# A mixture-of-experts and cosine block on one core: chains across engines spread over steps, conversions let in by a booked budget, the square on ScalarE

## The chip, the core and the metric

The kernel runs on one core of a Trainium2 chip. A core has a matrix engine (TensorE, PE in the rows; its weight loads are PEld), a vector engine (VectorE, DVE), an engine for activation functions (ScalarE, ACT), a general engine (GpSimd, POOL) and SyncE (SP), which here issues most transfers. Each engine takes its own instructions in order; a semaphore makes one wait for another. The metric is the time of one execution on the device in microseconds (us).

## The reference, cut to what matters

```python
scores = q @ k.T / 8 + bias            # 4 batches, 8 heads, 576 positions, 64 wide
x = softmax(scores) @ v                # -> 2304 tokens of 512
e = argmax(x @ w_gate)                 # one of 8 experts per token
y = gate * relu(x @ w1[e]) @ w2[e]     # 512 -> 1024 -> 512
h = y @ w_in                           # 512 -> 2048
out = (h * cos(h)) @ w_out             # 2048 -> 512
```

The weights `w_in` and `w_out` arrive as 64-bit floats and are turned into 32-bit ones on the chip.

## The kernel before

Three blocks follow each other: attention, the expert block (`moe_dense`), and the last block (`moe2`). To keep 32-bit precision each operand of a large product is split into a rounded high half (`h`) and a remainder, the low half (`l`), and a product is three matmuls: high by high, high by low, low by high.

**Expert block.** For each of the four batches `b` the expert that most of its tokens chose is applied to all of its 576 tokens; tokens of one other expert are gathered, computed apart and added (`Extra`). A batch has two halves `hf` of 288 tokens, a half eight hidden chunks `f`, so `seq` has 64 steps `s`. A step runs `layer1` of its chunk (12 matmuls into `pl`, of which there are two buffers, then ScalarE makes the high half `hh` and VectorE the low half `hl`) and `layer2` of the chunk two steps earlier (12 matmuls into `po`). Between them other work is issued, in a written-out order. `later.add` puts functions on step numbers, `later.step` runs those that are due, at the end of a step; `later.drip` takes single instructions out of a long chain of small ones (the gate's choice of experts, the choice of the extra group). That other work is:

- `split`: the high half of a quarter of a weight on ScalarE and at once its low half on VectorE, eight per batch.
- `split_x`: for the next half of tokens, the product of the activations with the gate factor `Cb` on GpSimd, the rounding on ScalarE, the subtraction on VectorE, all at once, two of four chunks at `f` = 3 and two at `f` = 4. For the very first half the product runs on VectorE, chunk by chunk, when the block opens.
- `cv.half`: half of the conversion of one piece of a 64-bit weight. The two halves of a piece are four VectorE instructions, then an addition on GpSimd and a transfer out. 40 pieces fall into this block, two halves in every step that a fixed condition lets through.
- `extra.add` (four steps per batch from step 48) adds the gathered tokens' result on VectorE; `split_group` at step 57 splits the first tokens of the last block.

**Last block.** Six groups `g` of 384 tokens, sixteen hidden chunks `f` each: 96 steps. A step runs `layer1` (12 matmuls into `ph`) and `layer2` of four steps earlier (9 matmuls into `py`). In between stands the chain of `h cos h`: ScalarE `turns` (the multiple of a full turn, `tk`), VectorE three instructions of `reduce` (L1267 to L1269), ScalarE the sine of half the angle (L1334), VectorE two instructions of `cosine` (L1274: -2 s s; L1275: (r + 1) h), ScalarE the high half `gh`, GpSimd the low half `gl` (L1344). The angle is taken at the step itself, reduction and sine one step later, the rest two steps later. In the first steps the second half of the weights (quarters 4 to 7) is still to be split: `split_w`, the high half on ScalarE, the low half on GpSimd. The next group's tokens are split at `f` = 8 to 11, the low half also on GpSimd.

## Time and profile before

| what | value |
|---|---|
| median of 3 runs | 1027.79 us (1026.69 to 1029.92) |
| the profiled execution | 1027.14 us, its span 1025.4 us |
| TensorE busy | 981.6 us, 96% of the span |
| VectorE, ScalarE, GpSimd busy | 780.5, 524.4, 363.0 us |
| mean granted TensorE clock | 0.986 |
| expert block, first matmul to the last block's first | 343.84 to 608.54 us |
| last block | from 608.54 us |

A row of the trace gives the line of the kernel, the engine, the operation, the tile written and those read (`hl<-pl,hh`), the shape, how often it came, and its times. The idle time of an engine stands in brackets with what ended it. A stretch's row gives each engine's busy time and number of instructions, the granted clock as a share of the full 2.4 GHz, and what transfers moved.

### The profile page before, as it was taken

What the parts mean: (1) busy time and instruction counts of PE and PEld (TensorE: products, weight loads), DVE (VectorE), ACT (ScalarE), POOL (GpSimd) and SP (SyncE); (2) the same over time, 40 slices, a digit from 0 to 9 for tenths busy, and PEclk for the clock granted to TensorE, in tenths of its full rate; (3) what the DMA queues carried; (4) which work ended last, traced back from release to release, by engine and by line L of the source; (5) the groups of instructions that cost most, each with busy time, mean ns of one, the idle gap of its engine ahead of it and who ended that gap; (6) DMA issues with size and microseconds to landing.
All of it is one profiled execution on the core that took longest, in us unless ns stands there. A gap on an engine that the chain in (4) does not pass through costs nothing. (4 is left out here: it accounts for less than half of the span.)

```text
span 1025.4 us, 17745 instructions
## 1 busy us (share of the span) xinstructions
PE 981.6 (96%) x6369; PEld 821.0 (80%) x6370; DVE 780.5 (76%) x1588; ACT 524.4 (51%) x1123; POOL 363.0 (35%) x408
## 2 busy tenths in 40 slices
PE   8989999999999898998999899999999999999996
PEld 4467777776666597998889897799999999999995
DVE  8977777778667578657448679988878779788774
ACT  8877878787776433325225355443334333333332
POOL 2655454556451122211212106733324224232221
PEclk9999999999999898999999999999999999999998
DMA  8974646664535384734556733101010010100000
GB/s 261 318 251 161 205 135 224 209 199 131 165 124 170 122 263 149 232 83 152 166 197 208 234 135 113 41 3 60 1 62 1 1 62 1 62 1 2 31 1 35
DMA packets 63886, 127.41 MB, mean 124 GB/s; under 512 B 6904, under 2 KB 21516, under 8 KB 63788
## 3 DMA queue, kind: packets, MB, share of 16 engines
q1 hardware_dynamic: 62860, 123.66, 37.1%
q0 software_dynamic: 640, 2.36, 0.8%
q8 instruction: 52, 0.85, 0.3%
q14 instruction: 46, 0.38, 0.1%
q10 hardware_dynamic: 288, 0.16, 0.1%
HBM read 92.55 MB, written 33.60 MB: 123 GB/s over the span
## 5 line engine op out<-in xcount | busy, mean ns | idle before, releaser
L1344 POOL TENSOR_TENSOR gl<-tg,gh 128x384 fp32r<-128x384 f32 x96 | 97.3, 1014 | 289.4 <-ACT gh L1343 289.3
L1262 ACT ACTIVATE tk<-ph,magic 128x384 f32<-128x384 f32 x96 | 55.6, 579 | 204.8 <-PE ph L1323 204.8
L1323 PE MATMUL ph<-xh,w0l 128*128 128x384 f32 x384 | 129.5, 337 | 0.0
L1323 PE MATMUL ph<-xh,w0h 128*128 128x384 f32 x384 | 129.2, 336 | 0.0
L1323 PE MATMUL ph<-xl,w0h 128*128 128x384 f32 x384 | 129.2, 336 | 0.0
L703 POOL TENSOR_TENSOR f32a<-f32a,raw 128x256 f32<-128x256 f32 x64 | 47.5, 742 | 205.9 <-DVE raw L701 120.1
L1269 DVE SCALAR_TENSOR_TENSOR tr<-tk,tr 128x384 f32<-128x384 f32 x96 | 116.6, 1215 | 3.3
L1358 PE MATMUL py<-w1h,gl 128*128 128x512 f32 x288 | 113.9, 395 | 3.0 <-POOL gl L1344 3.0
L1358 PE MATMUL py<-w1h,gh 128*128 128x512 f32 x288 | 113.5, 394 | 1.2 <-ACT gh L1343 1.2
L1358 PE MATMUL py<-w1l,gh 128*128 128x512 f32 x288 | 112.8, 392 | 0.0
L538 ACT ACTIVATE e<-s,mn 128x576 f32<-128x576 f32 x128 | 98.5, 770 | 20.0 <-DVE mn L527 17.3
L527 DVE CUSTOM_DVE_ANT_0 s<-ps_s,Bp 128x576 f32<-128x576 f32 x112 | 84.2, 753 | 30.6 <-PE ps_s L511 26.3
L596 PE MATMUL pa<-eT,V 128*64 128x256 f32 (+3 forms) x640 | 103.1, 425 | 0.6 <-ACT eT L565 0.6
L559 PE MATMUL Tp<-ident,e 128*128 128x128 f32 x576 | 87.4, 275 | 3.0 <-DVE eT L567 1.1
L824 PE MATMUL pl<-xh,w0h 128*128 128x288 f32 x256 | 82.1, 321 | 7.7 <-DVE hl L829 5.8
L510 PE MATMUL ps_s<-HI 128*128 128x288 f32 x256 | 84.2, 345 | 2.3 <-DVE mn L527 2.0
L1274 DVE SCALAR_TENSOR_TENSOR tr<-tr 128x384 f32<-128x384 f32 x96 | 82.2, 856 | 0.0
L824 PE MATMUL pl<-xl,w0h 128*128 128x288 f32 x256 | 78.0, 305 | 0.3
L510 PEld LDWEIGHTS ps_s<-HI 128*128 128x128 f32 x256 | 48.5, 189 | 36.7 <-issue 14.9
L824 PE MATMUL pl<-xh,w0l 128*128 128x288 f32 x256 | 77.3, 302 | 0.0
L842 PE MATMUL po<-hh,w1h 128*128 128x288 f32 x256 | 76.5, 299 | 0.0
L842 PE MATMUL po<-hl,w1h 128*128 128x288 f32 x256 | 76.4, 298 | 0.0
(213 smaller groups left out, 2473.0 us busy)
## 6 DMA issues: line engine op xcount, KB each, us to landing
Bp<-in_w SPq DMA_DIRECT2D x38, 512.0 KB, 4.7
Rqk<-in_qk SPq DMA_DIRECT2D x32, 576.0 KB, 6.1
Bd<-ev SPq DMA_DIRECT2D x36, 295.5 KB, 4.5
raw<-in_w_in SPq DMA_DIRECT2D x32, 256.0 KB, 4.4
raw<-in_w_out SPq DMA_DIRECT2D x32, 256.0 KB, 2.9
X<-xT SPq DMA_DIRECT2D x7, 1152.0 KB, 5.7
Bp<-Bd SPq DMA_DIRECT2D x21, 288.0 KB, 6.7
V<-in_v SPq DMA_DIRECT2D x16, 320.0 KB, 4.3
```

Source lines behind the costliest of these rows:

```text
L510: nc.tensor.matmul(ps[:, hf, :HF], w, HI[:, par, 1, sl], start=True, stop=False)
L527: nc.vector.tensor_tensor_reduce(out=h2(s), in0=d["ps"][:, :, :HF], in1=h2(bias(hp, i)), scale=-0.125, scalar=3e38, op0=ALU.add, op1=ALU.m ...
L538: nc.scalar.activation(out=e[:, par, :], in_=s, func=AF.Exp, bias=mn, scale=-1.0, accum_out=sm[b][:, qt, par, hp:hp + 1])
L559: nc.tensor.transpose(Tp[:, k, :], e[:, par, k * 128:(k + 1) * 128], ident)
L596: nc.tensor.matmul(pa[64 * par:64 * par + 64, :W], V[rows, k, par, :], eT[rows, k, par, :W], start=(k == 0), stop=(k == 4))
L824: nc.tensor.matmul(ps[:, :HF], w[:, c, :], x[:, c, :], start=(n == 0), stop=(n == 3 * NP_ - 1))
L842: nc.tensor.matmul(self.acc[d][:, :HF], w[:, ds_], x, start=(f == 0 and n == 0), stop=(f == self.FC - 1 and n == 2))
L1269: nc.vector.scalar_tensor_tensor(out=r, in0=k, scalar=-PI2B, in1=r, op0=ALU.mult, op1=ALU.add)
L1274: nc.vector.scalar_tensor_tensor(out=r, in0=r, scalar=-2.0, in1=r, op0=ALU.mult, op1=ALU.mult)
L1323: nc.tensor.matmul(ps[:, :GT], w[:, c, :], x[:, c, :], start=(n == 0), stop=(n == 3 * NP_ - 1))
L1344: nc.gpsimd.tensor_tensor(out=lo, in0=g, in1=hi.bitcast(F32), op=ALU.subtract)
L1358: nc.tensor.matmul(acc[t], x[:, ts_], w, start=(f == 0 and n == 0), stop=(f == FC - 1 and n == 2))
```

## The change

In the expert block `split` and `split_x` are cut into parts. The high half is issued in one step and the low half in the next. The product with the gate factor becomes a function of its own, `weigh`, on GpSimd, at `f` = 3 and 4 as before; rounding follows at `f` = 4, 5, subtraction at `f` = 5, 6. The first half's four products move into the last attention pair, on GpSimd. The conversions lose their fixed condition. Every piece of VectorE's work is booked in `dense.cost` with a written price, a half conversion of 0.73 is issued from step 3 on as long as the sum stays at or under `STEP` = 3.1, and 3.1 is taken off at the end of each step.

In the last block the low halves of the weights go to VectorE, one step behind the high half, and their loads and splits are three steps apart where they were two. The subtraction of the next group's tokens stays on GpSimd, a step after the rounding. The square runs on ScalarE after the sine; VectorE then makes (s s - 1/2) h in one instruction, and the output copies multiply by -2. Angle and reduction are issued a step after the first layer, sine and square two steps after it, cosine and split three; the second layer still follows four steps after the first. The output copy of each third of the tokens is issued straight after its matmuls.

```diff
@@ attention, last pair
+                if t - 15 * NTL in (2, 3, 4, 6):
+                    dense.weigh(0, 0, (2, 3, 4, 6).index(t - 15 * NTL), 1, nc.gpsimd)
@@ class Dense
-    def split(self, b, which, q):
-        nc = self.tc.nc
-        src = self.raw.pop((b, which, q))
+    def split(self, b, which, q, part=None):
+        nc = self.tc.nc
         hi, lo = self.w[which, q]
-        nc.scalar.activation(out=hi, in_=src, func=AF.Copy)
-        nc.vector.tensor_tensor(out=lo, in0=src, in1=hi.bitcast(F32), op=ALU.subtract)
+        src = self.raw[b, which, q]
+        if part != 1:
+            nc.scalar.activation(out=hi, in_=src, func=AF.Copy)
+        if part != 0:
+            nc.vector.tensor_tensor(out=lo, in0=src, in1=hi.bitcast(F32), op=ALU.subtract)
+            self.cost += 1.23
+            del self.raw[b, which, q]
...
+    def weigh(self, b, hf, c0, n, eng):
+        src = self.xT[:, c0:c0 + n, b, hf * HF:(hf + 1) * HF]
+        eng.tensor_tensor(out=src, in0=src, in1=self.gate.Cb[b][:, hf * HF:(hf + 1) * HF].unsqueeze(1).to_broadcast(
+            [128, n, HF]), op=ALU.mult)
...
-        (nc.vector if first else nc.gpsimd).tensor_tensor(
-            out=src, in0=src, in1=self.gate.Cb[b][:, t].unsqueeze(1).to_broadcast([128, n, HF]), op=ALU.mult)
-        nc.scalar.activation(out=hi, in_=src, func=AF.Copy)
-        nc.vector.tensor_tensor(out=lo, in0=src, in1=hi.bitcast(F32), op=ALU.subtract)
+        if part == 0:
+            nc.scalar.activation(out=hi, in_=src, func=AF.Copy)
+        else:
+            nc.vector.tensor_tensor(out=lo, in0=src, in1=hi.bitcast(F32), op=ALU.subtract)
+            self.cost += 0.38 * n
@@ moe_dense
+        def convert(least):
+            while cv and cv.u < cv.end and (dense.cost + 0.73 <= STEP or least > 0):
+                cv.half()
+                dense.cost += 0.73
+                least -= 1
...
-                if s < 5:
-                    dense.split(0, *((1, 1), (0, 2), (0, 3), (1, 2), (1, 3))[s])
-                if f in (3, 4) and (hf == 0 or b + 1 < B):
-                    dense.split_x(b + hf, 1 - hf, (f - 3) * 2, 2)
+                if hf == 0 or b + 1 < B:
+                    nx = b + hf, 1 - hf
+                    if f in (3, 4):
+                        dense.weigh(*nx, (f - 3) * 2, 2, nc.gpsimd)
+                    if f in (4, 5):
+                        dense.split_x(*nx, (f - 4) * 2, 2, 0)
+                    if f in (5, 6):
+                        dense.split_x(*nx, (f - 5) * 2, 2, 1)
...
+                dense.cost += 0.6 * bool(later.chains)
-            if cv and s >= 3 and s % 8 != 1 and not 19 <= s <= 23 and (s < 48 or s % 4 != 1):
-                cv.half()
-                cv.half()
+            if s >= 3:
+                convert(2 if s >= len(seq) else 0)
+            dense.cost = max(0.0, dense.cost - STEP)
@@ moe2
-            nc.gpsimd.tensor_tensor(out=lo, in0=src, in1=hi.bitcast(F32), op=ALU.subtract)
+            dense.split(B, which, q, 1)
...
+        def sines(s):
+            r = d[s]["r"]
             nc.scalar.activation(out=r, in_=r, func=AF.Sin, scale=0.5)
+            nc.scalar.activation(out=r, in_=r, func=AF.Square)
...
-            cosine(nc, g, d[s]["r"], d[s]["h"])
+            nc.vector.scalar_tensor_tensor(out=g, in0=d[s]["r"], scalar=0.5, in1=d[s]["h"], op0=ALU.subtract,
+                                           op1=ALU.mult)
...
-                        nc.scalar.activation(out=o, in_=acc[t], func=AF.Copy)
+                        nc.scalar.activation(out=o, in_=acc[t], func=AF.Copy, scale=-2.0)
...
-                    later.add([(2 * i + 2 + j, lambda q=q, j=j: dense.load(B, j, q, True))])
-                later.add([(2 * i + 4 + j, lambda q=q, j=j: split_w(q, j))])
+                    later.add([(3 * i + 1 + j, lambda q=q, j=j: dense.load(B, j, q, True))])
+                later.add([(3 * i + 3 + j + k, lambda q=q, j=j, k=k: split_w(q, j, k)) for k in range(2)])
...
-            later.step()
...
-                angles(s)
-            if 0 <= s - 1 < N:
-                reduced(s - 1)
-            if 0 <= s - 2 < N:
-                cosines(s - 2)
-                split_g(s - 2)
+            for lag, work in ((3, cosines), (1, angles), (1, reduced), (2, sines), (3, split_g)):
+                if 0 <= s - lag < N:
+                    work(s - lag)
+            later.step()
...
+                if f in (9, 10, 11, 12):
+                    lower_x(g + 1, f - 9)
```

## Rows read from the trace of the kernel before

**Rows 1.** Stretches, columns: length, busy PE, PEld, DVE, ACT, POOL; clock; transfer share; GB/s

```profile
343.84:608.54 264.70, 247.95 (x1754) 234.72 (x1755) 178.57 (x407) 96.75 (x187) 48.66 (x53) 0.96 0.56 181
...
621.07:662.06 40.99, 36.73 (x169) 29.54 (x168) 39.71 (x40) 19.91 (x34) 30.88 (x18) 1.00 0.31 96
662.06:1004.51 342.45, 342.45 (x1723) 310.96 (x1722) 283.13 (x424) 130.95 (x277) 106.26 (x101) 1.00 0.06 22
```

**Rows 2.** The same stretches, instructions on tile ph alone

```profile
621.07:662.06 40.99, 18.13 (x96) 17.04 (x96) 8.82 (x16) 4.49 (x8) 1.00 0.31 96
662.06:1004.51 342.45, 185.80 (x984) 174.61 (x984) 93.15 (x168) 48.26 (x83) 1.00 0.06 22
```

**Rows 3.** The chain that ended last, 585 to 600 us: start, us, what

```profile
589.71 1.58 PE pl L824 x12
591.29 1.59 PE po L842 x12
```

**Rows 4.** Waits of PE, expert block: us, times, longest

```profile
PE pl L824 <- DVE hl L829: 5.8, 5, 2.5
PE Tp L293 <- DVE cs L287: 4.3, 1, 4.3
PE Tp L1066 <- DVE xb L1060: 2.4, 1, 2.4
PE pl L824 <- ACT xh L797: 1.9, 4, 1.0
```

**Rows 5.** One stretch at the lower clock, as in rows 1

```profile
402.04:408.86 6.82, 6.82 (x31) 6.75 (x31) 6.61 (x16) 2.38 (x4) 1.48 (x2) 0.50 0.21 60
```

**Rows 6.** Waits of ACT and DVE in the expert block

```profile
ACT xh L797 <- POOL xT L795: 47.1, 12, 5.7
...
DVE xl L798 <- ACT xh L797: 30.7, 15, 3.2
```

**Rows 7.** Timeline, 563 to 566.5 us: start, us, engine, line, operation

```profile
563.75 1.42 POOL L795 TENSOR_TENSOR xT<-xT,Cb 128x576 f32<-128x576 f32 x1
...
565.21 0.69 ACT L797 ACTIVATE xh<-xT 128x576 fp32r<-128x576 f32 x1 [4.74 <-POOL xT L795]
...
565.93 0.76 DVE L798 TENSOR_TENSOR xl<-xT,xh 128x576 fp32r<-128x576 f32 x1 [2.65 <-ACT xh L797]
```

**Rows 8.** Timeline of DVE, 362 to 365 us: a conversion, then hl

```profile
362.55 0.29 DVE L694 TENSOR_SCALAR f32a<-raw 128x256 int32<-128x256 int32 x1
...
364.00 0.45 DVE L829 SCALAR_TENSOR_TENSOR hl<-pl,hh 128x288 fp32r<-128x288 f32 x1
```

**Rows 9.** DVE's costs by line in the expert block: busy us, mean ns

```profile
L782 DVE TENSOR_TENSOR w0l<-Bp,w0h 128x1024 fp32r<-128x1024 f32 x18 | 23.6, 1312 | 5.4 <-ACT w0h L781 5.3
```

**Rows 10.** Timeline, where the expert block opens

```profile
343.82 0.46 DVE L798 TENSOR_TENSOR xl<-xT,xh 128x288 fp32r<-128x288 f32 x1 [3.21 <-ACT xh L797]
...
344.19 0.45 DVE L795 TENSOR_TENSOR xT<-xT,Cb 128x288 f32<-128x288 f32 x1
...
345.15 0.46 DVE L798 TENSOR_TENSOR xl<-xT,xh 128x288 fp32r<-128x288 f32 x1 [0.51 <-ACT xh L797]
```

**Rows 11.** The page's 40 slices of the span, busy tenths

```profile
POOL 2655454556451122211212106733324224232221
```

**Rows 12.** Costs by line, DVE 662 to 1004.5 us, ACT from 608.54 us

```profile
L1274 DVE SCALAR_TENSOR_TENSOR tr<-tr 128x384 f32<-128x384 f32 x83 | 59.3, 715 | 0.0
...
L1334 ACT ACTIVATE tr<-tr 128x384 f32<-128x384 f32 x96 | 49.7, 517 | 9.7 <-DVE tr L1269 9.0
...
L1369 ACT ACT_TABLE_LOAD x1 | 1.3, 1283 | 0.0
```

**Rows 13.** Timeline, 638 to 643 us, in the last block's ramp

```profile
638.35 1.01 POOL L1344 TENSOR_TENSOR gl<-tg,gh 128x384 fp32r<-128x384 f32 x1 [1.71 <-ACT gh L1343]
...
639.32 2.72 POOL L1301 TENSOR_TENSOR w0l<-xc,w0h 128x1024 fp32r<-128x1024 f32 x1
...
639.70 2.76 DVE L1274 SCALAR_TENSOR_TENSOR tr<-tr 128x384 f32<-128x384 f32 x1
```

More of the change, by code (lines that the diff above doesn't have):

```diff
@@ L720, in __init__ @@
         self.raw, self.x, self.hid, self.acc = {}, {}, {}, None
-        self.group = None
+        self.group, self.cost = None, 0.0
     def open_early(self):
@@ L830, in layer1 @@
                                        op1=ALU.subtract)
+        self.cost += 0.45
         self.hid[b, hf, f] = hi, lo
@@ L864, in moe_dense @@
         for c in range(NP_):
-            dense.split_x(0, 0, c, 1, True)
+            for part in range(2):
+                dense.split_x(0, 0, c, 1, part)
         dense.split(0, 1, 0)
+        for s, (which, q) in enumerate(((1, 1), (0, 2), (0, 3), (1, 2), (1, 3))):
+            later.add([(s + 1 + k, lambda w=which, q=q, k=k: dense.split(0, w, q, k)) for k in range(2)])
         later.add(extra.parts(), X_AT)
@@ L874, in moe_dense @@
                 later.add([(W1_AT[b - 1] + 1, lambda b=b: gate.spread(b))])
-            later.add([(s0 + 10 + 2 * q, lambda b=b, q=q: dense.split(b, 0, q)) for q in range(4)])
-            later.add([(s0 + 13 + 2 * q, lambda b=b, q=q: dense.split(b, 1, q)) for q in range(4)])
+            for which in range(2):
+                later.add([(s0 + 10 + 3 * which + 2 * q + k, lambda b=b, w=which, q=q, k=k: dense.split(b, w, q, k))
+                           for q in range(4) for k in range(2)])
+        def convert(least):
[3 more added lines that the diff above has]
+                least -= 1
+        dense.cost = 0.0
         for s in range(len(seq) + LAG2):
@@ L891, in moe_dense @@
                 extra.add(a // 4, a % 4)
+                dense.cost += 1.0
                 if a % 4 == 3:
@@ L895, in moe_dense @@
                 extra.add(3, s - HALF_AT, slice(0, HF))
+                dense.cost += 0.5
                 if s == HALF_AT + NP_ - 1:
@@ L901, in moe_dense @@
                 dense.split_group()
+                dense.cost += 1.8
             if s < len(seq) + LAG2 - 1:
@@ L912, in moe_dense @@
             later.step()
+STEP = 3.1
 X_AT, X2_AT, ADD_AT, GROUP_AT, HALF_AT, NEXT_AT = 21, 34, 48, 57, 60, 61
@@ L1295, in moe2, with split_w @@
                 dense.tiles(wp, which, (q,))
-        def split_w(q, which):
-            src = dense.raw.pop((B, which, q))
-            hi, lo = dense.w[which, q]
-            nc.scalar.activation(out=hi, in_=src, func=AF.Copy)
-            nc.gpsimd.tensor_tensor(out=lo, in0=src, in1=hi.bitcast(F32), op=ALU.subtract)
+        def split_w(q, which, part):
+            if part == 0:
+                dense.split(B, which, q, 0)
+                return
+            dense.split(B, which, q, 1)
             for f in (2 * q, 2 * q + 1):
@@ L1311, in split_x, with lower_x @@
                 xsp[g] = dense.x_tiles()
-            hi, lo, src = xsp[g][0][:, c, :], xsp[g][1][:, c, :], xg[g][:, c, :]
-            nc.scalar.activation(out=hi, in_=src, func=AF.Copy)
-            nc.gpsimd.tensor_tensor(out=lo, in0=src, in1=hi.bitcast(F32), op=ALU.subtract)
+            nc.scalar.activation(out=xsp[g][0][:, c, :], in_=xg[g][:, c, :], func=AF.Copy)
+        def lower_x(g, c):
+            hi, lo = xsp[g]
+            nc.gpsimd.tensor_tensor(out=lo[:, c, :], in0=xg[g][:, c, :], in1=hi[:, c, :].bitcast(F32), op=ALU.subtract)
         def layer1(s):
@@ L1358, in layer2 @@
                     nc.tensor.matmul(acc[t], x[:, ts_], w, start=(f == 0 and n == 0), stop=(f == FC - 1 and n == 2))
-            if f == FC - 1:
-                for t in range(GT // 128):
+                if f == FC - 1:
                     o = op.tile([128, DM], F32, name="o")
                     if t % 2 == 0:
-                        nc.scalar.activation(out=o, in_=acc[t], func=AF.Copy)
+                        nc.scalar.activation(out=o, in_=acc[t], func=AF.Copy, scale=-2.0)
                     else:
-                        nc.vector.tensor_copy(out=o, in_=acc[t])
+                        nc.vector.tensor_scalar(out=o, in0=acc[t], scalar1=-2.0, scalar2=None, op0=ALU.mult)
                     nc.sync.dma_start(out=h["out"][g * GT + 128 * t:g * GT + 128 * t + 128, :], in_=o)
```

8 lines of the change are left out of this document (4 added, 4 removed).

## The prediction

> **What bounds the kernel now.** I read the busy times by stretch first, because the change touches only two stretches. Within the expert block TensorE is busy 247.95 of 264.70 us at a mean granted clock of 0.96, within the body of the last block 342.45 of 342.45, and in the last block's ramp, from its sixth step to its fourteenth, 36.73 of 40.99 [rows 1]. So TensorE is the bound in all three; what can be won is its idle time, its slow stretches and nothing else. Counting the first layer's matmuls gives steps: 96 in the ramp are 8 steps in 40.99 us, 5.12 each; 984 in the body are 82 steps in 342.45, 4.18 each [rows 2]. The ramp thus loses 40.99 - 8 x 4.18 = 7.6 us. An undisturbed expert step is 1.58 + 1.59 = 3.17 us [rows 3].
>
> The list of TensorE's waits says for whom: in the expert block hidden low halves from VectorE (5.8), one column sum from VectorE that the gate's chain waits for (4.3), the gathered low half from VectorE (2.4), and the first activations (1.9), 14.4 of the 16.75 idle [rows 4]. Each long one is followed by a stretch at half clock; one is 6.82 us at 0.50, the lower of the clock's two levels (1.2 of 2.4 GHz) [rows 5]. There are four (two of 6.82, two of 3.41), and the mean of 0.96 prices them: 0.04 x 264.7 = 10.6 us.
>
> Why is VectorE late? It is busy only 178.57 of 264.70 [rows 1], but it stands still for 30.7 us on the activations' high halves, and ScalarE for 47.1 on GpSimd's product before that [rows 6]. The timeline shows the relay: GpSimd multiplies (1.42), ScalarE rounds (0.69), VectorE subtracts after 2.65 us of standing still, all within one step of 3.17 [rows 7]. Engines run their queues in order, so the next hidden low half waits behind that, and the next first layer needs it because there are two accumulators.
>
> **Expert block, part by part.** Spreading the relay over steps: the product stays at f = 3, 4, the rounding goes to f = 4, 5, the subtraction to f = 5, 6. The same instructions, each behind one that has had a step to finish; the weights' splits are spread likewise. Nothing is added; what leaves VectorE's path is up to 30.7 us of standing still [rows 6]. The cost is slack: the last subtraction now ends two steps ahead of its use, where it had four. That cover holds as long as VectorE is under a step behind.
>
> The conversions: four VectorE instructions, two halves, run from 362.55 to 364.00, 1.45 us, 0.73 per half; a hidden low half is 0.45 [rows 8]. A weight subtraction is 1.31 [rows 9]. The old fixed list put two halves (1.45) beside 0.45 and 1.31 in the same step, 3.2, with an activation subtraction (0.76) and its standing still on top. The new rule adds 0.73 while the booked sum stays at or under 3.1. Counting it through the 64 steps: a bare step takes three halves (2.64), with the running chain two, with a split one, with split and subtraction none. After step 13 the old order has issued 20 halves and the new one 14; after step 30, 40 and 35; all 80 are out at step 54 before and step 63 now. The last block reads the first of these weights at steps 49 to 56, when 64 to 74 are done and at most 48 are needed, so no load waits for them. SyncE's queue carries the same transfers.
>
> The start: four chunks were made one after another, VectorE multiplying and subtracting in turn with ScalarE between, so the subtractions stand 345.15 - 343.82 = 1.33 us apart [rows 10]. With the products done on GpSimd in the last attention pair, they follow at about one subtraction, 0.46. Three intervals: 3 x (1.33 - 0.46) = 2.6 us, on the path. On GpSimd four products of half of 1.42 each [rows 7] are 2.8 us, in slices (13 and 14) where it is busy one tenth [rows 11]; behind them in its queue stand the small copies for the transposes, so if the gate factors came late attention would wait. A bound: none, or one product, 0.7, per copy, 2.8 in all; I take none.
>
> Sum: of the 12.5 us of waits on VectorE [rows 4] I take 11.5; of the short ones left (16.75 - 14.4 = 2.35) half, 1.2; the start 2.6; of the clock's 10.6, since its windows follow waits that go, 8.5. New waits where the rule counts too little are not in the trace; bound them below by none and above by what now stands there; I take 1.5. Together 11.5 + 1.2 + 2.6 + 8.5 - 1.5 = 22.3 us. Late next: TensorE itself.
>
> **Last block.** In the body no engine but TensorE sets the step. VectorE is busy 283.13 / 82 = 3.45 us per step [rows 1]; without the square (0.72, [rows 12]) 2.74. ScalarE has 130.95 / 82 = 1.60; a square like the sine is 0.52 [rows 12], so 2.12 of 4.18. The constant and the factor -2 ride on instructions that exist. This part is worth nothing in the body: TensorE hides it, and would stop hiding it only past 4.18.
>
> In the ramp the weights' low halves run on GpSimd, 2.72 us each, and VectorE's square begun beside one takes 2.76 where its mean in the body is 0.72 [rows 12, 13]. Eight of these go to VectorE at 1.31, issued one a step over steps 3 to 13, and the square that they blocked is gone: 2.74 + 1.31 = 4.05, under 4.18. Of the 7.6 us I take 7.0. The chain to the second layer is one step longer (the cosine at lag 3 where it was at 2), while the second layer still follows at lag 4. In the body four steps of 4.18 cover it; in the ramp's opening TensorE has only first layers to run in between, so some of the longer chain may show there. I leave 0.6 us for that. The output copies keep their order and their waits, so the end stays.
>
> On that price a rule weighs in. The row above shows VectorE held for the whole of a GpSimd operation. The Trainium skill says the same in SBUF — State Buffer, Who interferes with whom: the two share a port pair taken as an exclusive lock by a VectorE instruction with two SBUF inputs. A weight subtraction has two, so by it the eight moved ones would stand behind GpSimd's remaining operations; rival two works this out.
>
> **Total.** The profiled execution took 1027.14 us (span 1025.4). 1027.14 - 22.3 - 7.0 = 997.8; the median of the runs is 0.65 above that execution: **998.5 us**. If everything named goes (16.75 + 1.7 of hidden start + 10.6 + 7.6 = 36.6 us) it is 991.
>
> **Rivals.** *One: the rule counts too little.* The gate's chain is booked at 0.6 per step, and the gathers' subtractions, the selection and the four scale products not at all. Where those fall (steps 5 to 31) VectorE stays behind, and the waits for the column sum and the gathered half remain, 4.3 + 2.4 [rows 4], with the half-clock windows after them, 3.4 + 1.7 [rows 5]: 11.8 us back, 1010. For it: these steps hold most of the idle time. Against: by step 13 six halves, 4.4 us, fewer are queued and the standing still is gone.
>
> *Two: the lock follows the split.* Each of the eight weight subtractions waits for GpSimd's low half of 1.01 us [rows 13]: 2.74 + 1.31 + 1.01 = 5.06, 0.88 over the step, 8 times 7.0 us, less what three free steps give back (1.4 each): about 3 us, 1001.5. For it: the pair of rows in [rows 13]. Against: that low half takes GpSimd a quarter of a step, and the two need not meet.
>
> *Three: the waits are not VectorE's to give.* If TensorE's order itself (chains drained at once, gathers) makes the expert waits, only the last block gains: 1020.
>
> *Four, slower: the square needs another ScalarE table than the sine.* Then each step of the last block has two table loads, 2 x 1.28 [rows 12], and ScalarE needs 2.12 + 2.57 = 4.69 against 4.18: 0.51 x 96 = 49 us more, the ramp's 7.0 lost too, 1027.14 - 22.3 + 49 = 1054. It decides once ScalarE's extra exceeds 2.06 us per step. Against: the angle, the sine and the copy alternate now with one load in the whole block. The Trainium skill, in ScalarE: Activation LUTs, Table sets, says that tables load as named sets and that cheap functions are in every one; square is not among the four it names there. No run here shows a square.
>
> **How the numbers follow.** Forecast with rival two (992 to 1004): 0.66. Rival one (1004 to 1012): 0.18; rival three (1012 to 1024): 0.07; below 992: 0.02; no change: 0.02; slower: 0.05. The range 992 to 1012 holds 0.84 and takes in the bounds of the new waits. About 0.3%, 3 us, is what a measurement of this kernel can tell from no change: faster 0.92, same 0.03, slower 0.05.
>
> **What would show it.** Right: TensorE's idle time in the expert block under 5 us, no half clock after the column sum's place, VectorE's standing still for high halves under 5; in the ramp steps of 4.2 and no VectorE operation above 2.3 us. Wrong: waits for hidden low halves at steps 24 to 31 (rival one), weight subtractions of 2.3 in the ramp (two), more than one table load in the last block (four).

## The result, and the profile after

| | before | after |
|---|---|---|
| median of 4 runs beside each other | 1027.34 us (1026.69 to 1029.92) | 999.66 us (997.34 to 1002.51) |
| ratio, 95% interval | | 0.9727 (0.9697 to 0.9758) |
| span of the profiled execution | 1025.40 us | 1000.68 us |
| attention, to the expert block's first matmul | 343.84 | 348.23 |
| expert block | 264.70 | 240.08 |
| last block, steps 0 to 4 | 12.53 | 13.23 |
| ramp, steps 5 to 12 | 40.99 | 33.59 |
| body, 82 steps | 342.45 | 342.45 |
| last matmuls | 12.48 | 12.48 |
| from the last matmul to the end | 8.41 | 10.63 |

The forecast was 998.5 us. The two stages that the change aims at gave 24.62 us and 7.40 - 0.70 = 6.70 us, 31.3 together where 29.3 was forecast; the median fell by 27.7. The profiled execution of after happens to be the longest of its four, and its attention and its end are 4.39 and 2.22 us longer than before's. Both come from places that the change hardly touches: two stretches at half clock early in the attention (10.24 and 3.41 us, against one of 3.41 before), and the last output transfers, which took 4.2 us from issue to landing (2.0 before). Other kernels with the same attention code took 343.3 to 348.5 us in it, and the kernels that issue their output copies as after does ended 7.9 to 10.6 us after the last matmul. So I compare stage by stage.

The stretches of after, in the columns of [rows 1]: the expert block, steps 0 to 4, the ramp, the body.

```profile
348.23:588.31 240.08, 237.14 (x1755) 227.79 (x1756) 184.90 (x402) 97.83 (x187) 52.03 (x52) 0.99 0.61 199
588.31:601.54 13.23, 12.87 (x72) 11.99 (x71) 11.67 (x19) 10.47 (x19) 1.32 (x2) 1.00 0.17 56
601.54:635.13 33.59, 33.59 (x170) 30.34 (x169) 32.10 (x45) 25.34 (x47) 15.85 (x13) 1.00 0.35 118
635.13:977.57 342.44, 342.44 (x1723) 310.96 (x1722) 169.30 (x335) 170.22 (x355) 99.42 (x98) 1.00 0.07 22
```

The second number of a row is TensorE's busy time. In the ramp it now equals the length, in the expert block 2.94 us are missing where 16.75 were. So TensorE is the bound in every stretch, and nearly all of its idle time is gone. VectorE does about the same work in the expert block (184.90 against 178.57 us) and three fifths of it in the body (169.30 against 283.13).

TensorE's waits in the expert block of after (us in total, times, longest), to be set against [rows 4]:

```profile
PE pl L838 <- ACT xh L809: 1.0, 1, 1.0
PE Tp L1037 <- issue: 0.9, 1, 0.9
PE Tp L293 <- DVE cs L287: 0.8, 1, 0.8
PE po L857 <- DVE w1l L787: 0.7, 1, 0.7
```

The hidden low halves (5.8) and the gathered low half (2.4) are not in the list any more, and the column sum's wait fell from 4.3 to 0.8. Behind it VectorE and ScalarE, to be set against [rows 6]:

```profile
DVE hl L843 <- ACT hh L842: 25.5, 28, 5.5
DVE f32a L696 <- DMA Wo<-f32a: 8.4, 5, 4.5
...
DVE xl L811 <- ACT xh L809: 3.8, 1, 3.8
...
ACT xh L809 <- POOL xT L797: 6.4, 4, 2.2
```

VectorE's standing still on the activations' high halves fell from 30.7 us to 3.8, and those 3.8 are a single wait at the block's opening, which ends as TensorE begins. Most of what is left is idle for the right reason: 25.5 us (36.0 before) for hidden high halves that TensorE has not yet made possible. The second row has grown: the conversions wait for a transfer out of a buffer, of which there are two, 8.4 + 2.6 us in all, where the kernel before has 1.4.

What is left of half clock is one stretch (PEclk 0.50, the lower of the two levels, 1.2 of 2.4 GHz), where before had four with 20.48 us in all:

```profile
400.61:404.02 3.41, 3.41 (x16) 3.41 (x16) 3.41 (x6) 1.36 (x2) 0.51 (x1) 0.50 0.34 112
```

In the last block, the costs by line: VectorE in the body, then ScalarE in the whole block, to be set against [rows 12].

```profile
L1305 DVE SCALAR_TENSOR_TENSOR tr<-tk,tr 128x384 f32<-128x384 f32 x83 | 49.8, 599 | 2.9
L1304 DVE SCALAR_TENSOR_TENSOR tr<-tk,ph 128x384 f32<-128x384 f32 x82 | 45.5, 555 | 2.8
L1382 DVE SCALAR_TENSOR_TENSOR tg<-tr,ph 128x384 f32<-128x384 f32 x82 | 44.8, 547 | 0.0
...
L1378 ACT ACTIVATE tr<-tr 128x384 f32<-128x384 f32 x96 | 50.6, 527 | 3.0
L1377 ACT ACTIVATE tr<-tr 128x384 f32<-128x384 f32 x96 | 49.6, 516 | 3.2 <-DVE tr L1305 3.1
L1413 ACT ACT_TABLE_LOAD x1 | 1.3, 1283 | 0.0
```

96 sines (L1377) alternate with 96 squares (L1378), and the table is loaded once. A square takes 527 ns, a sine 516.

### The profile page after: what moved, and what is told of

Same layout as the page of the kernel before. It is cut to its first block, busy times and chain, and to the rows that moved or that the text cites. A ratio compares the mean times of both kernels' runs of the same rounds, so it can differ in the third digit from the quotient of the medians.

```text
span 1000.7 us, 17705 instructions
## 1 busy us (share of the span) xinstructions
PE 969.3 (97%) x6369; PEld 819.0 (82%) x6370; DVE 660.3 (66%) x1496; ACT 573.9 (57%) x1219; POOL 352.0 (35%) x404
## 4 chain that ended last, share of the span: by engine, by line
PE 87%; DVE 6%; DMA 3%; ACT 2%; issue 1%; SPq 0%; POOL 0%; DVEq 0%; ACTq 0%; POOLq 0%
PE py L1403 20%; PE ph L1363 19%; PE pa L596 9%; PE pl L838 8%; PE po L857 8%; PE Tp L559 6%; PE ps_s L510 5%; PE ps_s L511 3%; PE ps L389 3%; DVE hhD L379 1%; PE ps_s L515 1%; DMA F<-Fd 1%; DMA Bd<-ev 1%; PE ps_s L516 1%; PE Tp L1135 1%
## 5 line engine op out<-in xcount | busy, mean ns | idle before, releaser
L1303 DVE TENSOR_SCALAR tk<-tk 128x384 f32<-128x384 f32 x96 | 36.8, 384 | 155.0 <-ACT tk L1298 154.8
L705 POOL TENSOR_TENSOR f32a<-f32a,raw 128x256 f32<-128x256 f32 x64 | 48.6, 760 | 208.6 <-DVE raw L703 188.4
L538 ACT ACTIVATE e<-s,mn 128x576 f32<-128x576 f32 x128 | 98.6, 770 | 24.6 <-DVE mn L527 23.1
L842 ACT ACTIVATE hh<-pl 128x288 fp32r<-128x288 f32 x64 | 26.3, 412 | 100.7 <-PE pl L838 97.6
L838 PE MATMUL pl<-xh,w0h 128*128 128x288 f32 x256 | 79.0, 309 | 1.0 <-ACT xh L809 1.0
L857 PE MATMUL po<-hh,w1l 128*128 128x288 f32 x256 | 76.0, 297 | 0.7 <-DVE w1l L787 0.7
L838 PE MATMUL pl<-xl,w0h 128*128 128x288 f32 x256 | 75.6, 295 | 0.2 <-DVE xl L811 0.2
```

The costliest lines, as they stand in the source:

```text
L538: nc.scalar.activation(out=e[:, par, :], in_=s, func=AF.Exp, bias=mn, scale=-1.0, accum_out=sm[b][:, qt, par, hp:hp + 1])
L705: self.tc.nc.gpsimd.tensor_tensor(out=af[:], in0=af[:], in1=low, op=ALU.add)
L838: nc.tensor.matmul(ps[:, :HF], w[:, c, :], x[:, c, :], start=(n == 0), stop=(n == 3 * NP_ - 1))
L857: nc.tensor.matmul(self.acc[d][:, :HF], w[:, ds_], x, start=(f == 0 and n == 0), stop=(f == self.FC - 1 and n == 2))
```

## The experiments

Twelve kernels, each with the stage lengths of its profile. "Idle" and "half" are TensorE's idle time (the length less its busy time) and its time at half clock within the expert block.

| kernel | median us | ratio to before (95%) | expert | idle | half | steps 0 to 4 | ramp | body |
|---|---|---|---|---|---|---|---|---|
| before | 1027.34 | | 264.70 | 16.8 | 20.5 | 12.53 | 40.99 | 342.45 |
| after | 999.66 | 0.9727 (0.9697 to 0.9758) | 240.08 | 2.9 | 3.4 | 13.23 | 33.59 | 342.45 |
| e4, expert block alone | 1004.61 | 0.9765 (0.9741 to 0.9789) | 240.55 | 3.4 | 3.4 | 12.53 | 42.36 | 342.45 |
| e5, last block alone | 1020.03 | 0.9928 (0.9909 to 0.9946) | 264.42 | 16.4 | 20.5 | 12.53 | 33.59 | 342.45 |
| e1, fixed list of conversions | 1002.49 | 0.9751 (0.9735 to 0.9768) | 244.90 | 6.5 | 0.0 | 12.59 | 33.59 | 342.45 |
| e2, relay in one step | 998.53 | 0.9722 (0.9695 to 0.9749) | 241.79 | 3.3 | 6.8 | 13.24 | 33.59 | 342.45 |
| e9, both of these | 1011.63 | 0.9861 (0.9829 to 0.9894) | 255.68 | 12.0 | 13.7 | 12.59 | 33.58 | 342.45 |
| e3, weights' halves in one step | 1000.88 | 0.9749 (0.9705 to 0.9793) | 241.51 | 5.2 | 0.0 | 12.53 | 33.59 | 342.45 |
| e8, opening's products on VectorE | 1001.25 | 0.9768 (0.9725 to 0.9810) | 242.42 | 2.7 | 6.8 | 13.23 | 33.59 | 342.45 |
| e10, the budget alone | 1007.27 | 0.9813 (0.9793 to 0.9834) | 248.65 | 8.1 | 6.8 | 12.53 | 33.59 | 342.45 |
| e6, low halves on GpSimd | 997.57 | 0.9733 (0.9689 to 0.9776) | 236.98 | 1.8 | 0.0 | 13.22 | 33.59 | 342.45 |
| e7, square on VectorE | 999.05 | 0.9748 (0.9713 to 0.9784) | 237.41 | 1.7 | 0.0 | 12.51 | 33.83 | 343.51 |
| e11, both of these | 1003.50 | 0.9789 (0.9757 to 0.9822) | 237.33 | 2.1 | 0.0 | 12.53 | 38.64 | 344.77 |
| e12, last block's old order | 994.74 | 0.9677 (0.9643 to 0.9711) | 238.58 | 2.9 | 0.0 | 13.25 | 33.59 | 342.45 |

Six of these profiles have the changed expert code word for word (after, e4, e6, e7, e11, e12). They show the block at 236.98 to 240.55 us, with no or one stretch at half clock. A difference of less than some 3.5 us between two profiles of the expert block thus proves nothing; the idle column is the steadier one. Less half of the time at half clock, the six lie closer together, at 236.98 to 238.84 us. By that measure e1 stands 6 to 8 us above them and e3 some 3 to 4.5, while e2 lies among them and e8 at most 2 above.

**e4 and e5: the two blocks apart.** The changed expert block with the old last block, and the reverse.

```diff
e4:
-def moe2(...)            # as after
+def moe2(...)            # as before
e5:
-class Dense, moe_dense, attention   # as after
+class Dense, moe_dense, attention   # as before, but for the parts of split that moe2 calls
```

> The change in the attention and expert blocks alone; the last block as before. Theory (the two blocks gain apart from each other): the expert block takes 240 us as in the changed kernel, the last block's ramp is back at 41 us for steps 5 to 13; 1027.3 - 24.6 = 1003 us. Rival (VectorE's leftovers from the expert block are what slows the ramp): the ramp is shorter than 41 us by itself and the time is nearer 998.

> The change in the last block alone; attention and expert block as before. Theory: the expert block keeps its 264.7 us, the ramp's steps 5 to 13 take 34.3 us instead of 41.0; 1027.3 - 6.7 = 1020.6 us. Rival (the ramp gains only because the expert block leaves VectorE free): little gain, 1026 or more.

Measured by stages: e4 has after's expert block and before's ramp, 1.4 us longer, e5 before's expert block, to its 20.5 us of half clock, and after's ramp. The blocks gain nearly apart from each other: 1027.5 - 1004.6 = 22.9 and 1027.5 - 1020.0 = 7.5 us. They do touch a little: e4's ramp is 1.4 us longer only beside the new expert block, and so is the opening of after by 0.7 (its cause stands in the next section).

**e1 and e2: the budget and the spread of the relay, each undone.**

```diff
e1:
-            if s >= 3:
-                convert(2 if s >= len(seq) else 0)
+            if cv and s >= 3 and s % 8 != 1 and not 19 <= s <= 23 and (s < 48 or s % 4 != 1):
+                cv.half()
+                cv.half()
e2:
-                    if f in (4, 5):
-                        dense.split_x(*nx, (f - 4) * 2, 2, 0)
-                    if f in (5, 6):
-                        dense.split_x(*nx, (f - 5) * 2, 2, 1)
+                    if f in (3, 4):
+                        dense.split_x(*nx, (f - 3) * 2, 2, 0)
+                        dense.split_x(*nx, (f - 3) * 2, 2, 1)
```

> The changed kernel with the fixed list of conversions (two halves in most steps) instead of the booked budget. Theory (both parts count, the standing still more: 30.7 us of VectorE's time against 6 halves of 0.73 that come earlier): the expert block takes about 247 us, 7 more than in the changed kernel; 1006 us. Rival A (the conversions' number per step is what made VectorE late): 256 us or more, 1016. Rival B (the spread relay alone is enough): under 242 us, 1001.

> The changed kernel with product, rounding and subtraction of the next activations in one step again (f = 3 and 4); budget and spread weights stay. Theory: VectorE stands still for some 30 us again, and the expert block takes about 253 us, 13 more than in the changed kernel; 1013 us. Rival A (with the budget VectorE has room to stand still): under 244 us, 1003 at most. Rival B (the relay is the whole of it): 262 us or more, 1022.

e1 lost 4.8 us, less than the 7 that I had expected. e2 lost 1.7 us of the block, less than profiles of the same code differ by, and nothing of the kernel's time. My theory for e2 fell and its rival A came true: the relay's standing still, on which the prediction rests [rows 6, 7], is not worth 13 us by itself. Without the budget the spread saves most of the gain, without the spread the budget saves nearly all.

**e9: both undone.** It keeps the spread of the weights and the products ahead of the block, so that it tells whether those two carry the gain.

```diff
# the edits of e1 and e2 together
```

> The changed kernel with two parts of the expert block undone together: the hand-written list of the conversions' steps and the relay of the activations in one step. The spread of the weights' splits and the products computed ahead of the block stay. Theory (either of the two cures is enough by itself, because a conversion and a relay must meet in one step for VectorE to stand still): the expert block takes 256 to 261 us, against 240.1 with both cures, 244.9 without the budget and 241.8 without the relay's spread; VectorE waits for the activations' high halves 20 us or more and the kernel takes 1012 to 1018 us. Rival (most of the gain is in the weights' spread and in the block's start, which were kept in both runs): the block stays under 248 us and the kernel under 1006 us.

The block went to 255.68 us, 15.6 above after, where e1 and e2 had lost 4.8 and 1.7. That is 0.3 under what I had expected, and the kernel's 1011.63 us is 0.4 under. So the two stand in for each other; neither is idle. Of the 9.1 us that the undoings cost more together than apart, some 5 are idle time of TensorE (9.1 more than after in e9, 3.6 in e1, 0.4 in e2), most of the rest half clock. The waits of e9 are nearly those of [rows 4, 6] again, but for the column sum's: TensorE, VectorE, ScalarE.

```profile
PE pl L838 <- DVE hl L843: 5.0, 5, 2.5
PE Tp L1102 <- DVE xb L1096: 2.1, 1, 2.1
...
DVE xl L811 <- ACT xh L809: 30.9, 13, 3.8
...
ACT xh L809 <- POOL xT L797: 43.2, 13, 6.1
```

Its timeline shows what VectorE stands still for, in the two relays of one half (start, us, engine, line, operation, in brackets the idle time before it and what ended that):

```profile
553.86 0.43 DVE L703 SCALAR_TENSOR_TENSOR raw<-raw,f32p 128x256 f32<-128x256 uint32 x1
554.21 0.45 DVE L843 SCALAR_TENSOR_TENSOR hl<-pl,hh 128x288 fp32r<-128x288 f32 x1
554.42 0.75 POOL L705 TENSOR_TENSOR f32a<-f32a,raw 128x256 f32<-128x256 f32 x1 [4.43 <-DVE raw L703]
555.13 1.42 POOL L797 TENSOR_TENSOR xT<-xT,Cb 128x576 f32<-128x576 f32 x1
...
556.59 0.69 ACT L809 ACTIVATE xh<-xT 128x576 fp32r<-128x576 f32 x1 [4.74 <-POOL xT L797]
...
557.30 0.76 DVE L811 TENSOR_TENSOR xl<-xT,xh 128x576 fp32r<-128x576 f32 x1 [2.65 <-ACT xh L809]
...
561.51 0.74 POOL L705 TENSOR_TENSOR f32a<-f32a,raw 128x256 f32<-128x256 f32 x1 [4.96 <-issue]
562.21 1.41 POOL L797 TENSOR_TENSOR xT<-xT,Cb 128x576 f32<-128x576 f32 x1
...
564.37 0.76 DVE L811 TENSOR_TENSOR xl<-xT,xh 128x576 fp32r<-128x576 f32 x1 [2.62 <-ACT xh L809]
```

The relay begins with VectorE itself. GpSimd's product (L797) stands in its queue behind the addition of a conversion (L705), and that waits for VectorE's last conversion instruction (L703). Only then do 0.70 of addition, 1.42 of product and 0.69 of rounding run, while VectorE, whose only other work is one hidden low half of 0.45, stands still for 2.65 us at the subtraction. It is the same 2.65 as in [rows 7]. The second relay stands behind a conversion in the same way. The same two relays in e2, with the budget:

```profile
542.60 0.75 POOL L705 TENSOR_TENSOR f32a<-f32a,raw 128x256 f32<-128x256 f32 x1 [10.19 <-DVE raw L703]
...
543.30 2.82 POOL L797 TENSOR_TENSOR xT<-xT,Cb 128x576 f32<-128x576 f32 x2
...
545.49 1.25 DVE L811 TENSOR_TENSOR xl<-xT,xh 128x576 fp32r<-128x576 f32 x1 [2.04 <-ACT xh L809]
...
546.16 0.69 ACT L809 ACTIVATE xh<-xT 128x576 fp32r<-128x576 f32 x1
...
547.39 1.21 DVE L787 TENSOR_TENSOR w1l<-Bp,w1h 128x1024 fp32r<-128x1024 f32 x1
548.53 0.44 DVE L843 SCALAR_TENSOR_TENSOR hl<-pl,hh 128x288 fp32r<-128x288 f32 x1
...
548.89 0.74 DVE L811 TENSOR_TENSOR xl<-xT,xh 128x576 fp32r<-128x576 f32 x1
```

Here no conversion stands between the two products (one row, x2). The first subtraction still waits 2.04 us. The second product follows the first at once, its rounding is done while VectorE has a weight's low half to make, and the second subtraction waits for nothing. Of the block's 14 relays VectorE stands still for 2 us or more in ten in e9 and in one in e2. Over the block e2 waits 12.2 us for high halves against 30.9 in e9, 3.8 of them at the opening in both. What it still waits falls where VectorE has room: no hidden low half is left in the list of TensorE's waits. The budget takes conversions out of full steps, the spread takes the subtraction out of the wait. With the budget and no spread of the relay (e2) no hidden low half is late. With the spread and no budget (e1) seven still are, 4.0 us in all, but by 1.1 at the most where it is 2.5 in e9, and no half clock follows them.

**e3, e8 and e10: the rest of the expert block.** The weights' halves in one step; the opening's products on VectorE; and both of these with e2's edit, so that of the expert block's change the budget alone is left.

```diff
e3:
-            later.add([(s + 1 + k, lambda w=which, q=q, k=k: dense.split(0, w, q, k)) for k in range(2)])
+            later.add([(s + 1, lambda w=which, q=q: dense.split(0, w, q))])
...                      # the same for batches 1 to 4
e8:
-                if t - 15 * NTL in (2, 3, 4, 6):
-                    dense.weigh(0, 0, (2, 3, 4, 6).index(t - 15 * NTL), 1, nc.gpsimd)
...
+            dense.weigh(0, 0, c, 1, nc.vector)
             for part in range(2):
                 dense.split_x(0, 0, c, 1, part)
e10:
# the edits of e2, e3 and e8 together
```

> The changed kernel with both halves of an expert weight's split in one step again, the rest as changed. Theory (the weights' spread matters little, since VectorE waits for ScalarE's weight half of 0.7 us and no longer): the expert block takes 240 to 242 us and the kernel within 2 us of the changed one. Rival (it is the weights' spread that freed VectorE): the block takes 246 us or more, and the kernel 1004 us or more.

> The changed kernel with the first half's four products on VectorE at the block's start again, instead of on GpSimd during the attention. Theory (the opening is bound by VectorE's chain): the first layer-1 group takes 4.5 to 5.5 us instead of 2.3, the half clock that followed the opening comes back, and the expert block is 3 to 5 us longer, 243 to 245 us; the kernel takes 1002 to 1005 us. Rival (the opening was short because of the spread of the weights, not because of the products): the block stays under 241.5 us.

> The changed kernel with three of the expert block's four changes undone: the relay in one step, the weights' halves in one step and the products of the start on VectorE; what stays of the expert block's change is the conversions let in by the budget. Theory (the budget alone keeps conversions and relays apart, and the other cures add only the start): the expert block takes 244 to 248 us, with under 15 us in which VectorE waits for the activations' high halves, and the kernel takes 1002 to 1007 us. Rival (the cures hold only together, and what was undone one at a time was covered by the others): the block takes 252 us or more.

e3 raised TensorE's idle time from 2.9 to 5.2 us, three waits for hidden low halves (3.3 us in all) among it; the kernel's time didn't move beyond its interval. Its profile has no half clock, so the block's 241.51 is to be set against the 237 to 239 of after's code without one: the weights' spread is worth some 3 to 4.5 us. The theory's 240 to 242 was set by after's 240.08, which has 1.7 us of half clock in it. In e8 the first twelve matmuls took 5.35 us again, as before, where after takes 2.28, and a stretch at half clock (348.4 to 351.8) followed. The block is 242.4, 0.6 under what I expected: 2.3 over after, whose profile has one stretch at half clock where e8 has two, and 4 to 5 over the 237 to 239 us of profiles without one. The kernel's 1001.25 us is under the 1002 that I had expected and lies among the times of after. e10 missed both bounds: 248.65 us, between the 244 to 248 of the theory, by 0.65, and the 252 of the rival, with 18.5 us of standing still where I had said under 15. The budget alone thus gives 264.70 - 248.65 = 16.1 of 24.6 us, everything but the budget (e1) 19.8. The four edits, undone one at a time, show 4.8 + 1.7 + 1.4 + 2.3, some 10 us of 24.6, and as they stand only the 4.8 is more than profiles of the same code differ by: single undoings don't add up here. Whether the relay's spread and the weights' spread also stand in for each other was not run by itself.

**e6, e7 and e11: what cured the ramp.** The weights' low halves back on GpSimd; the square back on VectorE; both.

```diff
e6:
-            dense.split(B, which, q, 1)
+            src = dense.raw.pop((B, which, q))
+            hi, lo = dense.w[which, q]
+            nc.gpsimd.tensor_tensor(out=lo, in0=src, in1=hi.bitcast(F32), op=ALU.subtract)
e7:
-            nc.scalar.activation(out=r, in_=r, func=AF.Square)
...
-            nc.vector.scalar_tensor_tensor(out=g, in0=d[s]["r"], scalar=0.5, in1=d[s]["h"], op0=ALU.subtract,
-                                           op1=ALU.mult)
+            cosine(nc, g, d[s]["r"], d[s]["h"])
...                      # and the factor -2 out of the output copies
e11:
# the edits of e6 and e7 together
```

> The changed kernel with the low halves of the last block's eight weight chunks on GpSimd again, the square of the sine still on ScalarE and the work still spread over steps. Theory (the ramp was lost to GpSimd's subtractions of 2.72 us, which delay the activations' low half of 1.0 us and hold VectorE back): steps 5 to 12 take 37 to 41 us instead of 33.6, the kernel 1003 to 1007 us, and the long VectorE operations of 2 us and more come back in the ramp. Rival (the ramp was lost to VectorE's two operations of the cosine, and the move of the square is what cured it): steps 5 to 12 stay within 33.6 to 34.6 us and the kernel within 1 us.

> The changed kernel with the square of the sine on VectorE again (the cosine's two operations as before), the weights' low halves kept on VectorE and the spread over steps kept. Theory (either of the two moves is enough, since VectorE's square is long only beside GpSimd's subtractions of 2.7 us): steps 5 to 12 take 33.6 to 35 us, VectorE's square takes 0.55 to 1.3 us, the body stays at 342.4 us and the kernel within 2 us of the changed one. Rival (the square's place is what cured the ramp, since the ramp did not lengthen when the low halves went back to GpSimd): steps 5 to 12 take 36 us or more.

> The changed kernel with both moves of the last block undone, the square on VectorE and the weights' low halves on GpSimd, but the chain still spread over the steps (the sine a step behind the reduction, the low halves a step behind the high ones). Theory (the ramp was VectorE's square held up by GpSimd's subtractions): steps 5 to 12 take 37 to 41 us, VectorE's square takes 2 us or more in them, and the kernel takes 1002 to 1007 us. Rival (what cured the ramp is the spread of the chain over steps, which both earlier runs kept): steps 5 to 12 stay under 34.6 us and the kernel within 1 us of the changed one.

e6 went to its rival: the ramp is 33.59 with the low halves on GpSimd. e7 went to its theory, 33.83, with 1.06 us more in the body, in its second and third step. With both undone the loss is back: 38.64 in the ramp and 2.32 in the body, together 383.41 us, as before the change (40.99 + 342.45 = 383.44). So either move is enough, and the spread of the chain, which e11 keeps, gives nothing against before. Against e4, which has e11's expert block and the old chain, it is 1.4 us (42.36 + 342.45 = 384.81). In e11, VectorE's square in the ramp by its line, GpSimd's subtractions, and one pair from the timeline:

```profile
L1310 DVE SCALAR_TENSOR_TENSOR tr<-tr 128x384 f32<-128x384 f32 x9 | 19.1, 2119 | 0.0
...
L1341 POOL TENSOR_TENSOR w1l<-xc,w1h 128x1024 fp32r<-128x1024 f32 x3 | 8.2, 2730 | 0.0
...
597.84 2.73 POOL L1341 TENSOR_TENSOR w1l<-xc,w1h 128x1024 fp32r<-128x1024 f32 x1
598.22 2.77 DVE L1310 SCALAR_TENSOR_TENSOR tr<-tr 128x384 f32<-128x384 f32 x1
```

The square is held until GpSimd's subtraction ends, [rows 13] again: 2.12 us in the mean, where the same square without such a neighbour takes 0.64 in e7's ramp. In e6, without the square, GpSimd's subtractions hold another operation, the rounding `tk` (by its line, and one pair):

```profile
L1303 DVE TENSOR_SCALAR tk<-tk 128x384 f32<-128x384 f32 x10 | 12.6, 1264 | 6.6 <-ACT tk L1298 6.6
...
609.48 2.72 POOL L1341 TENSOR_TENSOR w1l<-xc,w1h 128x1024 fp32r<-128x1024 f32 x1
...
610.32 2.10 DVE L1303 TENSOR_SCALAR tk<-tk 128x384 f32<-128x384 f32 x1
```

There the holding costs TensorE nothing: VectorE is busy 27.19 of 33.58 us and even waits 6.6 us for ScalarE. The ramps of e11, e6 and e7, in the columns of [rows 1]:

```profile
594.38:633.03 38.65, 36.13 (x170) 29.66 (x168) 37.34 (x41) 18.22 (x33) 26.29 (x17) 1.00 0.33 102
597.21:630.79 33.58, 33.58 (x169) 30.34 (x168) 27.19 (x37) 25.00 (x46) 29.29 (x20) 1.00 0.37 118
594.57:628.41 33.84, 33.84 (x170) 30.10 (x168) 32.53 (x46) 18.23 (x33) 12.02 (x11) 1.00 0.36 117
```

Over eight steps VectorE, the time in which it is held included, has 4.96 us of work per step before (39.71) and 4.67 in e11 (37.34), both over TensorE's 4.18, and the steps took 5.12 and 4.83; in e7 it has 4.07, in after 4.01, in e6 3.40, all under. The ramp was a matter of this sum, not of the holding as such.

**e12: the old order of the chain, with both moves.**

```diff
+            later.step()
...
-            for lag, work in ((3, cosines), (1, angles), (1, reduced), (2, sines), (3, split_g)):
+            for lag, work in ((0, angles), (1, reduced), (1, sines), (2, cosines), (2, split_g)):
...
-            later.step()
...
-                if f in (9, 10, 11, 12):
-                    lower_x(g + 1, f - 9)
+                if f in (8, 9, 10, 11):
+                    lower_x(g + 1, f - 8)
```

> The changed kernel with the order of the last block's chain as before (rounding in layer 1's own step, sine and square in the reduction's step, cosine and its halves a step later, activations' low halves in the step of their high ones), both moves kept: the square on ScalarE, the weights' low halves on VectorE. Theory (the moves of work carry the ramp, the spread only shifts when each link is issued): steps 5 to 12 take 33.6 to 35 us, the opening step that took 4.9 us takes 4.2 again, and the kernel is within 1.5 us of the changed one. Rival (the spread carries the 2.3 us by which the ramp stayed shorter than before when both moves were undone, 38.6 against 41.0, and is needed beside them): steps 5 to 12 take 36 us or more.

The ramp is 33.59, so the spread isn't needed beside the moves either. The opening step stayed at 4.9 us, which I had expected to go, and the kernel is not within 1.5 us of the changed one: its median is the lowest of all, 994.74 us. But in the last block not a stage differs from after by more than 0.03; what differs is the half clock, in the attention and the expert block, and the end after the last matmul (7.9 against 10.6). The two intervals overlap, so I don't call it faster than after.

## Why the prediction came out right, step by step

**Expert block, 22.3 us forecast, 24.6 measured.** The clock's term was 8.5 us; 20.48 us at half clock became 3.41, and half of the difference is 8.5. That it fits to the tenth is chance: four of the six profiles of after's code show no half clock in the block, two show 3.41. The waits on VectorE less the new ones were put at 11.5 - 1.5 = 10.0; the list has 12.5 before [rows 4] and 0.8 + 0.7 + 0.2 after, so 10.8. The new waits of 1.5 are the weight's low half (0.7) and little else. The other waits fell from 16.75 - 12.5 = 4.2 to 2.94 - 1.7 = 1.2, by 3.0 where 1.2 were counted; 1 us of it is the opening's. Idle time thus fell by 13.8 in all. That opening was sized at 2.6; the first twelve matmuls fell from 5.35 to 2.28, 3.1 us, of which some 0.9 is the half clock that begins within them and counted already. Idle time and clock make 22.3; the remaining 2.3 us are in neither. Some 0.8 of them lie in the first two steps, where TensorE is shown as busy in matmuls of 0.4 and 0.6 us that start one by one behind VectorE; for the other 1.5 I have no rows.

**The reason was half right.** VectorE's standing still was named as the cause, and the spread of the relay as its cure. The place was right; e2 shows that the cure was not the only one. The prediction said how the old list overfilled a step, but gave the budget no gain of its own and put "up to 30.7 us" beside the spread. In fact the budget alone gives 16.1 of 24.6 us (e10); what the other three edits add together is 8.6, and the relay's spread, with these in place, nothing that shows (e2). The total survived this, since it was taken from the waits and not from the edits.

**The bound on the conversions.** The prediction saw no new wait in them. VectorE waits 8.4 + 2.6 us for the transfers out of the two conversion buffers, because the budget lets several halves follow each other. TensorE's list has no wait for them.

**Last block, 7.0 forecast, 6.7 measured.** The ramp gave 7.40 of 7.6, and the opening cost 0.70 where 0.6 was left for it. The size left for the opening was luck, as the cause is another one (below). The sum of 4.05 us of VectorE per step came out at 32.10 / 8 = 4.01, but not by its terms: six and not eight of the weights' subtractions fall in these steps (they are issued at steps 4 to 14, not 3 to 13), and they take 1.78 us in the mean and not 1.31. The body was forecast at nothing and moved by 0.01. VectorE's part of its step was put at 2.74 and is 169.30 / 82 = 2.06, because the last of the three reduction instructions, which I had counted as it was, got shorter too (1.25 us before, 0.60 after). It has two operands from SBUF. In the body before, 79 of 84 of them start while a GpSimd operation runs, in after's body 5 of 82; with the square back on VectorE it is 84 of 84 and 1.28 us again (e7, e11), with the old order of the chain it stays short (e12). So the square's move took VectorE out of GpSimd's way in nearly every step, which TensorE hides. ScalarE's part was put at 2.12 and is 2.08. The reading that the ramp needs both the low halves and the square moved was too strong: e6 and e7 show that one suffices. The opening's 0.7 us is in after, e2, e6, e8 and e12 and in no other kernel. It doesn't come from the spread of the chain, for which the prediction had left 0.6 (e12 has the old order and keeps it). The trace of after shows the wait:

```profile
590.15 2.35 DVE L787 TENSOR_TENSOR w1l<-Bp,w1h 128x1024 fp32r<-128x1024 f32 x2
592.60 1.05 ACT L1298 ACTIVATE tk<-ph,magic 128x384 f32<-128x384 f32 x2 [1.22 <-DVE w1l L787]
...
598.75 1.01 POOL L1389 TENSOR_TENSOR gl<-tg,gh 128x384 fp32r<-128x384 f32 x1 [10.12 <-ACT gh L1388]
...
599.81 0.19 PEld L1403 LDWEIGHTS py<-w1h,gl 128*128 128x128 f32 x1 [0.79 <-POOL gl L1389]
```

TensorE reaches its first second-layer matmuls and waits for the first low half `gl`. Two things must meet for that. VectorE comes late out of the expert block: two of the last weight's subtractions still stand before the first angle, and the first reduction starts 4.90 us after the block's first matmul, where it is 3.57 with one subtraction left (e3, e5, e10) and 4.25 in e1 and e9. And two squares stand in ScalarE's queue before the first high half `gh`: from that reduction to the end of `gl` it is 6.55 us, and 5.78 where VectorE makes the square. Late and long, `gl` ends 11.46 us after the first matmul (after); long only, 10.12 (e3); late only, 10.69 (e7), and neither of these two has the wait. The price comes out of the expert block's change and the square together.

**The rivals.** *One*, the rule counts too little: the waits that it wanted to keep, 4.3 and 2.4, are 0.8 and none. The booking is coarse, as it said, but e1 shows that beside the spread even the fixed list costs 4.8 us only. Of its clock something is left: the 3.41 us at half clock stand 2 us behind the column sum's wait, at 398.3, so my sign "no half clock there" failed in this profile; e6, e7, e11 and e12 have the same wait of 0.5 to 0.8 and no half clock. *Two*, the lock follows the split: it does, and costs nothing. The timeline of after in the ramp:

```profile
618.91 1.03 POOL L1389 TENSOR_TENSOR gl<-tg,gh 128x384 fp32r<-128x384 f32 x1 [2.19 <-ACT gh L1388]
618.96 2.05 DVE L787 TENSOR_TENSOR w0l<-xc,w0h 128x1024 fp32r<-128x1024 f32 x1
...
619.89 2.01 POOL L1354 TENSOR_TENSOR xl<-xg,xh 128x384 fp32r<-128x384 f32 x1
```

The weight's subtraction started beside GpSimd's low half and took 2.05 us, where an undisturbed one takes 1.21; six of the eight in the last block took 2.04 to 2.08. TensorE waits for none: the free steps between pay for it, where the rival had left 3 us. The Trainium skill, SBUF — State Buffer, Who interferes with whom, calls the shared port pair an exclusive lock that goes to whichever instruction is issued first. The trace agrees in both directions: GpSimd's next operation, started while VectorE's subtraction ran, took 2.01 us where 16 of the 20 of its line take 1.01 to 1.02. *Three*, the waits are not VectorE's to give: dead with the list of waits, and e9, which brings VectorE's waits back, brings 15.6 us back. *Four*, the table: one load.

## What to carry to other kernels

When an engine stands still in a relay that it started itself (its own result, another queue, a third engine, and back), either give it other work in between or take the return trip into a later step; see by undoing both whether one would do. Count a gain from the waits that end, not from the edits that are to end them: here the four edits covered for each other, and undone one at a time they showed at most some 10 of 24.6 us. And where two engines hold each other up, add the holding to the held one's work per step and set the sum against the step: at 3.40 to 4.07 us of 4.18 the holding cost nothing, at 4.67 and 4.96 it did.

## What the runs showed of the hardware that I had not expected

GpSimd's subtraction holds not only VectorE's operations with two operands from SBUF. The rounding `tk` (L1303), one operand and a constant, took 0.35 us alone and up to 2.23 beside it (e6). A square on ScalarE needs no table of its own beside the sine: 96 of each, one load, 0.53 us a piece. And the clock's half stretches vary between profiles of the same code: the expert block had none or one of 3.41 us in six of them, which alone moves it by 1.7 us.
